# Attention and a token/channel mixer on one core: paced loads, moved squares, merges on another engine, another order at the start

## The chip, the cores and the metric

The kernel runs on one core of a Trainium2 chip. A core has TensorE (PE, matrix products), VectorE (DVE), ScalarE (ACT), GpSimd (POOL) and SyncE (SP, used here only to issue transfers); 16 DMA engines move data between the chip's memory and the core. TensorE reads from the on-chip SBUF and writes to PSUM, which has eight banks of 512 float32 values in each of 128 partitions. The metric is the device time of the program in microseconds (us).

## The reference

Eight batches of 576 positions, eight heads of 64. First causal attention with a bias that comes from `s`, then a mixer over tokens and one over channels:

```python
scores = scale * np.matmul(q, k.transpose(0, 1, 3, 2))
cum = np.cumsum(np.maximum(s, 0.0), axis=-1)
bias = -(cum[:, :, :, None] - cum[:, :, None, :])
scores = np.where(causal, -1000000000.0, scores + np.minimum(bias, 0.0))
attn = softmax(scores); x = np.matmul(attn, v)          # heads side by side: (8, 576, 512)
h  = np.maximum(xt @ w_tok1, 0.0) @ w_tok2              # xt: x with tokens last; 576 -> 256 -> 576
u  = x + h.transpose(0, 2, 1)
h2 = np.maximum(u @ w_ch1, 0.0) @ w_ch2                 # 512 -> 1536 -> 512
out = u + h2
```

## The kernel before

Because the bias is a difference of cumulative sums, the kernel multiplies v by weights exp(cum - cum_end / 2) (tile `wT`) and adds a column of those weights for the denominators; distant blocks of keys, whose weight is negligible, are left out. The program checks the data for this (cumulative sums in `gaps`, and sums of squares of all q and k in `square`), sums the flags, and runs a general version behind a branch if one is set.

The work of one batch `b`:

- `load_cast` and `stage_v`: q, k and v are loaded by POOL's queue (`load_op`), q and k with a cast to bf16 in two halves of four heads into a ring of five tiles `qkn`, v in five pieces of 128 positions into one of two tiles `vf`. All loads form one chain in the program's order, and each waits for the landing of the load eight before it.
- `merge_v` (L631): each piece of v times its weights, into `vp`; `ones` (L640, L642) copies the weight column. For batch one on VectorE, for batch two on either engine, for the other six on POOL.
- `quad` (L689): TensorE transposes q and k of four heads, and VectorE or ScalarE copies them out of PSUM (L699, L701). `pair` (L731): scores, exp on ScalarE (L739), the causal mask on VectorE (L748, L756), products with v on TensorE (L802), division (L831, L835). Batch one has its mask instead from presets (L722), matmuls that write large negative numbers into the score banks first.
- `tok` (L899, L961): the token mixer; from batch three on, its result `ua`, `ub`, `us` is transposed into `uTa`, `uTb` by transposing transfers on SyncE's queue (L977). `chan` (L1017, L1042): the channel mixer, with relu evictions on ScalarE (L1024) or VectorE (L1026), and stores (L1055, L1058).
- `squares` (L647): sums of squares on ScalarE. The tiles of batches one and two are given up before their squares can be taken, so `stage_sq` loads those q and k again, eight more loads at the end of the chain.

The order is not that of the text: every step is an operation with a duration for each engine that may run it, and `Plan.run` places operations one by one on engines and buffers by readiness and priority, with its own model of the load stream (`dma_free`, the time at which the first transfer can begin, and a length for each load). After 50 us of planned time it adds 0.5 us to what TensorE waits for and 2 us to what waits for a transfer. Each engine then executes its list strictly in that order. Before 45 us of planned time gaps on TensorE are filled with matmuls on zeros (L1135). Two score buffers `psc` (two banks each) and four single banks `pmx` hold all of TensorE's results.

At the very start the k and q of the first four heads come through SyncE's queue, are cast on ScalarE and VectorE and transposed; s comes third, VectorE takes its scan (L534, `cum`), ScalarE the exponential `wn` (L540), TensorE turns it (L560), and VectorE copies it to `wT` (L564) and merges v.

In the program as built, the kernel has 6,854 TensorE instructions ahead of the general version's, matmuls and weight loads together.

Of the kernel before, what the change touches and what calls it, by code (L numbers as in the profile page):

```python
# [13 lines left out]

SWITCH = 0.095
# [39 lines left out]
class Plan:  # L55
# [11 lines left out]
    def op(self, alts, reads=(), writes=(), prio=0, dma=0.0, holds=(), after=None, mode=0, lock=False, alone=None):  # L67
        o = Op()
        o.alts = alts
        o.prio = prio  # L70
        o.dma = dma
        o.mode = mode
        o.lock = lock
        o.alone = alone
        o.idx = len(self.ops)
        o.deps = set()
        o.users = []
        o.bufs = []
# [24 lines left out]
        self.ops.append(o)  # L103
        return o

    def run(self, eps=0.03):
# [15 lines left out]
        dma_free = 6.0  # L122
# [20 lines left out]
        while left:  # L143
# [68 lines left out]
            for u in o.users:  # L212
# [6 lines left out]
                else:  # L219
                    rdy = fin  # L220
                    if fin > STEADY:
                        rdy += MARGIN_DMA if o.dma else MARGIN if u.alts.keys() == {"PE"} else 0.0
# [145 lines left out]
def kernel(  # L368
# [83 lines left out]
    def load_op(fn, key, us, occ=0.75, prio=-1):  # L452
# [7 lines left out]
    def load_cast(n, b, h, i, src):  # L460
# [4 lines left out]
        load_op(load, [(n, i)], 1.45, prio=-1 if b or h else -3)  # L465
# [50 lines left out]
    for ti, src in enumerate((k, q)):  # L516
# [17 lines left out]
    P.op({"DVE": (1.3, 1.6, lambda: nc.vector.tensor_tensor_scan(  # L534
        out=cum[:, :], data0=one_sb[:, :], data1=s_sb[:, :], initial=0.0, op0=ALU.mult, op1=ALU.add))},
        reads=["sr"], writes=["cum"], prio=-1)
# [62 lines left out]
    def stage_v(b, cs=tuple(range(NJ))):  # L599
# [4 lines left out]
        for c in cs:  # L604
# [13 lines left out]
            load_op(load, [(vf, c)], 1.15 * n / 128, 0.92)  # L618
# [3 lines left out]
    def merge_v(b, cs=tuple(range(NJ))):  # L622
        vf, vp = vbuf[b]
        odd = b % 2
        for c in cs:
# [17 lines left out]
        P.op({"POOL": (0.5, 0.7, lambda: ones(nc.gpsimd))} if b else {"DVE": (0.25, 0.3, lambda: ones(nc.vector))},  # L643
             reads=["wT"], writes=[(vp, "w")], prio=b * 10 + 5 if b else -5, lock=True)
# [27 lines left out]
    def quad(b, h):  # L672
# [4 lines left out]
        for ti in range(2):  # L677
# [6 lines left out]
            def tr(ti=ti, pv=pv):  # L684
                for r in range(R):
# [6 lines left out]
            P.op({"PE": (R * 0.031, R * 0.031 + 0.21, tr)}, reads=([(nat, ti, 0), (nat, ti, 1)] if b == 0 and h == 0 else [(nat, ti)]) + ["ident"] + pads,  # L692
                 writes=[(pts[e], e) for e in range(2)], holds=[d[ti] for d in dsts], prio=(np_ - 30 * (b < 1 and h < 1), 2), mode=1)
# [13 lines left out]
    def pair(b, h, kT, qT):  # L707
# [3 lines left out]
        for pc, piece in enumerate(PIECES):  # L711
# [7 lines left out]
            if b == 0:  # L719
# [4 lines left out]
                P.op({"PE": (2 * c_pe(512)[0], 2 * c_pe(512)[0] + 0.21, preset)}, reads=["neg", "ident"],  # L724
# [116 lines left out]
    def load_w(fn, key, us, occ=0.75):  # L841
        load_op(lambda: nc.gpsimd.dma_start(**fn()), [key], us, occ)
# [246 lines left out]
    for b in range(2):  # L1089
        for h in range(0, H, 4):  # L1090
            stage_sq(b, h)
    for b in range(B):
# [3 lines left out]
        chan(b, *st)  # L1096

# [86 lines left out]
```

## Time and profile before

| | |
|---|---|
| median of three runs | 306.04 us (305.45 to 306.58) |
| the profiled execution | 306.06 us, span of its instructions 304.3 us |
| TensorE, VectorE, ScalarE, POOL busy in the span | 96%, 57%, 60%, 35% |
| granted TensorE clock | 0.995 |
| read from the chip's memory, written to it | 40.65 MB, 9.44 MB |

Lines of the profile name the kernel's line, the engine and operation, and the tiles without buffer numbers (`pmx<-uTb,wc`). POOLq and SPq are queues that issue transfers; a transfer's landing is later than its issue. Times in the timeline count from the first instruction of the span. "issue" is time in which an engine waited for nothing that the profile shows.

### The profile page before, as it was taken

The numbers are of one execution on the slowest core, as the hardware profiler recorded it, in microseconds if no ns is written. First come the engines' busy times: TensorE is split into PE (matmuls) and PEld (weight loads), VectorE is DVE, ScalarE is ACT, GpSimd is POOL, SyncE is SP. The second block draws the span as 40 slices with busy tenths as digits, with TensorE's granted clock in tenths as the row PEclk, the third lists the DMA queues.
The fourth block names the chain that finished last, engine by engine and source line by source line (L and its number), as shares of the span: only waits on it lengthen the run. The fifth ranks groups of instructions, "written<-read, shape, count | busy, mean of one in ns | idle before, by whom it ended". The sixth has DMA issues, their size and how long they took to land.

```text
span 304.3 us, 8094 instructions
## 1 busy us (share of the span) xinstructions
PE 291.8 (96%) x3430; PEld 168.2 (55%) x3430; DVE 172.0 (57%) x368; ACT 182.8 (60%) x298; POOL 107.6 (35%) x147
## 2 busy tenths in 40 slices
PE   8899999899999999999999999998999999999991
PEld 3478566467754545457754545455764544457550
DVE  5962889377976456756556556956456642420030
ACT  5887884699996486609872387727761286017300
POOL 8675469999780418107620108500000000000000
PEclk9999999999999999999999999999999999999998
DMA  8999999999997673358455535894004310250032
GB/s 218 226 207 206 216 224 229 252 190 262 227 156 125 155 197 54 79 140 178 94 80 103 133 84 83 132 116 136 2 2 84 125 38 0 69 155 2 0 111 74
DMA packets 38348, 39.29 MB, mean 129 GB/s; under 512 B 17600, under 2 KB 30976, under 8 KB 38304
## 3 DMA queue, kind: packets, MB, share of 16 engines
q0 software_dynamic: 17072, 24.25, 44.6%
q1 hardware_dynamic: 21232, 14.44, 18.7%
q8 instruction: 29, 0.48, 0.7%
q14 instruction: 15, 0.12, 0.1%
HBM read 40.65 MB, written 9.44 MB: 165 GB/s over the span
## 4 chain that ended last, share of the span: by engine, by line
PE 84%; DMA 12%; POOL 1%; issue 1%; DVE 0%; POOLq 0%
PE pmx L1017 30%; PE pmx L1042 30%; PE pmx L961 5%; PE pmx L899 5%; PE psc L802 5%; PE psc L731 5%; DMA qkn<-in_k_dram 5%; PE psc L689 3%; DMA wc<-in_moe_w_ch_dram 3%; DMA vf<-in_v_dram 2%; DMA uTb<-us 2%; POOL qkn L462 1%; PE pmx L986 0%; DVE of L1050 0%; POOL keep masks.py:66 0%
## 5 line engine op out<-in xcount | busy, mean ns | idle before, releaser
L1017 PEld LDWEIGHTS <-wc 128*128 128x128 bf16 x624 | 57.9, 98 | 32.6 <-issue 1.5
L739 ACT ACTIVATE E<-psc 128x1024 bf16<-128x1024 f32 x64 | 62.2, 1024 | 22.8 <-PE psc L731 22.2
L1017 PE MATMUL pmx<-uTb,wc 128*128 128x320 bf16 (+2 forms) x384 | 56.1, 299 | 1.4 <-DMA uTb<-ub 1.1
L1042 PE MATMUL pmx<-wc,gb 128*128 128x512 bf16 (+1 forms) x252 | 55.3, 369 | 0.0
L1017 PE MATMUL pmx<-uTa,wc 128*128 128x512 bf16 (+1 forms) x240 | 45.6, 337 | 0.0
L647 ACT ACTIVATE junk<-qkn 128x1152 bf16<-128x1152 bf16 x32 | 37.3, 1166 | 11.7 <-DMA qkn<-in_q_dram 11.3
L1042 PE MATMUL pmx<-wc,ga 128*128 128x512 bf16 x192 | 44.1, 379 | 0.0
L631 POOL TENSOR_TENSOR vp<-vf,wT 128x512 bf16<-128x512 f32 (+1 forms) x31 | 32.3, 1058 | 25.6 <-PE psc L802 24.9
L1024 ACT ACTIVATE gb<-pmx 128x320 bf16<-128x320 f32 (+2 forms) x57 | 24.7, 438 | 21.2 <-PE pmx L1017 17.3
L1042 PEld LDWEIGHTS <-gb 128*128 128x128 bf16 x252 | 23.6, 98 | 24.8 <-issue 0.2
L613 POOL DMA_DIRECT2D vf<-in_v_dram x39 | 34.1, 884 | 7.3 <-DMA qkn<-in_k_dram 2.2
L748 DVE TENSOR_TENSOR E<-E,keep 128x512 bf16<-128x512 bf16 x56 | 25.8, 474 | 13.3 <-ACT E L739 13.1
L1042 PEld LDWEIGHTS <-ga 128*128 128x128 bf16 x192 | 18.2, 98 | 20.4
L1024 ACT ACTIVATE ga<-pmx 128x512 bf16<-128x512 f32 (+1 forms) x36 | 19.2, 535 | 11.7 <-PE pmx L1017 11.1
L462 POOL DMA_DIRECT2D qkn<-in_k_dram x19 | 14.1, 744 | 33.5 <-issue 31.8
L1026 DVE TENSOR_SCALAR gb<-pmx 128x320 bf16<-128x320 f32 (+2 forms) x39 | 18.8, 487 | 11.9 <-PE pmx L1017 11.5
L699 ACT COPY kT<-psc 128x576 bf16<-128x576 bf16 x22 | 13.1, 641 | 19.4 <-PE psc L689 17.9
L802 PEld LDWEIGHTS <-E 128*128 128x128 bf16 x576 | 21.1, 97 | 5.5
L835 DVE TENSOR_TENSOR x<-psc,rc 128x640 bf16<-128x640 f32 x28 | 23.0, 823 | 0.9
L1050 DVE TENSOR_TENSOR of<-pmx,ua 128x512 f32<-128x512 f32 x16 | 11.0, 689 | 19.5 <-PE pmx L1042 19.3
L731 PE MATMUL psc<-qT,kT 64*128 64x256 bf16 (+2 forms) x320 | 21.3, 250 | 0.0
L731 PEld LDWEIGHTS <-kT 64*128 64x128 bf16 x320 | 12.6, 94 | 14.6 <-issue 11.5
(107 smaller groups left out, 300.9 us busy)
## 6 DMA issues: line engine op xcount, KB each, us to landing
vf<-in_v_dram POOLq DMA_DIRECT2D x32, 256.0 KB, 7.9
out_dram<-of SPq DMA_DIRECT2D x31, 256.0 KB, 2.3
qkn<-in_k_dram POOLq DMA_DIRECT2D x19, 288.0 KB, 6.7
qkn<-in_q_dram POOLq DMA_DIRECT2D x19, 288.0 KB, 7.3
wc<-in_moe_w_ch_dram POOLq DMA_DIRECT2D x8, 384.0 KB, 11.4
out_dram<-of SPq DMA_DIRECT2D x10, 128.0 KB, 2.3
vf<-in_v_dram POOLq DMA_DIRECT2D x7, 128.0 KB, 7.4
gb<-in_k_dram SPq DMA_DIRECT2D x1, 576.0 KB, 3.9
```

Of the source, the lines that this page charges most:

```text
L613: nc.gpsimd.dma_start(out=vf.t[p0 : p0 + n, c, :, :], in_=v[b, :, c * 128 : c * 128 + n, :].rearrange("h p d -> p h d"))
L631: eng.tensor_tensor(out=vp.t[p0 : p0 + n, c, :, 0:D], in0=vf.t[p0 : p0 + n, c, :, :], in1=wT[p0 : p0 + n, cw, b * H : b * H + H].unsqueeze ...
L647: nc.scalar.activation(out=junk[:, :].rearrange("p (t n) -> p t n", t=2), in_=i, func=AF.Square, accum_out=sq[:, col : col + 1])
L731: nc.tensor.matmul(out=ps.t[:, hh * 512 + c0 : hh * 512 + c0 + e - a], lhsT=kT.t[hh * 64 : hh * 64 + 64, j0 : j0 + 128], rhs=qT.t[hh * 64 ...
L739: nc.scalar.activation(out=E.t[:, :, 512 * pc : 512 * pc + 512], in_=ps.t[:, :].rearrange("p (e n) -> p e n", e=2), func=AF.Exp, scale=0.125)
L748: nc.vector.tensor_tensor(out=o, in0=o, in1=keep[:, :].unsqueeze(1).unsqueeze(1).to_broadcast([128, 2, 2, 128]), op=ALU.mult)
L802: nc.tensor.matmul(out=o[:, ic, 0:DE], lhsT=E.t[:, hh, d0 : d0 + 128], rhs=vp.t[:, jc, h + 2 * hh, 0:DE], start=(jc == j_lo), stop=(jc == ic))
L835: nc.vector.tensor_tensor(out=x.t[:, :, :].rearrange("p c (g f e d) -> p g e f c d", f=2, e=2, d=D)[:, h // 4, h % 2], in0=pav2()[:, :, :, ...
L1017: nc.tensor.matmul(out=pm.t[:, 0 : e - a], lhsT=wc1[:, m, cc * 128 : cc * 128 + 128], rhs=uT.t[:, m, a:e], start=(m == 0), stop=(m == NMC ...
L1024: lambda cc=cc, pm=pm, a=a, e=e: nc.scalar.activation(out=g.t[:, cc, a:e], in_=pm.t[:, 0 : e - a], func=AF.Relu),
L1026: lambda cc=cc, pm=pm, a=a, e=e: nc.vector.tensor_scalar_max(out=g.t[:, cc, a:e], in0=pm.t[:, 0 : e - a], scalar1=0.0)),
L1042: nc.tensor.matmul(out=pm.t[:, na:ne], lhsT=g.t[:, cc, c * 128 : c * 128 + 128], rhs=wc2[:, cc, na:ne], start=(cc == 0), stop=(cc == NCC - 1))
```

## The change

Five edits, after which the planner orders everything anew:

1. Loads 17 to 44 of the chain are each preceded on POOL by a one-element copy (`touch`) from the tile that the load five before it fills, so that at most five are under way. The first of these is a part of `w_ch2`, right behind the loads of token weights, of `w_ch1` and of the first half of batch two.
2. The eight extra loads for squares leave the end of the chain as built and come behind five such copies that read the five columns of `uTb` of batch six (index 5), each filled by one of its transposing transfers. Squares get 6 us more of planned margin behind their loads, the copies none.
3. For batches three to eight, v is merged by VectorE and not by POOL, the weight columns too; batch two may still use either for the merges.
4. The presets of batch one wait for the first transposes; the scan of s waits for the second ones, with a lower priority.
5. The planner takes 6.85 instead of 6.0 us as the earliest begin of the load stream.

```diff
+DEPTH = 5
+PACED = (16, 44)
...
-        dma_free = 6.0
+        dma_free = 6.85
...
-                        rdy += MARGIN_DMA if o.dma else MARGIN if u.alts.keys() == {"PE"} else 0.0
+                        m = MARGIN_DMA + u.late if o.dma else MARGIN if u.alts.keys() == {"PE"} else 0.0
+                        rdy += max(m, 0.0)
...
+    def touch(ap, reads, col):
+        o = P.op({"POOL": (0.12, 0.2, lambda: nc.gpsimd.tensor_copy(out=seen[0 : ap().shape[0], col : col + 1], in_=ap()))},
+                 reads=reads, writes=[("seen", col)], prio=-1, after=chain[-1])
+        o.late = -9.0
+        chain.append(o)
+
+    probes = []
+
+    def load_op(fn, key, us, occ=0.75, prio=-1, probe=None):
+        if PACED[0] <= len(probes) < PACED[1]:
+            touch(*probes[-DEPTH], 0)
+        probes.append((probe, key))
...
-    P.op({"DVE": (1.3, 1.6, lambda: nc.vector.tensor_tensor_scan(
+    scan = P.op({"DVE": (1.3, 1.6, lambda: nc.vector.tensor_tensor_scan(
...
-        reads=["sr"], writes=["cum"], prio=-1)
+        reads=["sr"], writes=["cum"], prio=2)
...
-            alts = {} if b == 0 else {"POOL": (*c_pool(512, 0.0019), lambda mul=mul: mul(nc.gpsimd))}
-            if b < 2:
-                alts["DVE"] = (*c_dve(512), lambda mul=mul: mul(nc.vector))
-            P.op(alts, reads=[(vf, c), "wT"], writes=[(vp, c)], prio=-2 if b < 3 else b * 10 + 5, lock=True)
+            alts = {"DVE": (*c_dve(512), lambda mul=mul: mul(nc.vector))}
+            if b == 1:
+                alts["POOL"] = (*c_pool(512, 0.0019), lambda mul=mul: mul(nc.gpsimd))
+            P.op(alts, reads=[(vf, c), "wT"], writes=[(vp, c)], prio=-2 if b < 3 else b * 10 + 5, lock=b < 2)
...
-        P.op({"POOL": (0.5, 0.7, lambda: ones(nc.gpsimd))} if b else {"DVE": (0.25, 0.3, lambda: ones(nc.vector))},
-             reads=["wT"], writes=[(vp, "w")], prio=b * 10 + 5 if b else -5, lock=True)
+        P.op({"POOL": (0.5, 0.7, lambda: ones(nc.gpsimd))} if b == 1 else {"DVE": (0.3, 0.35, lambda: ones(nc.vector))},
+             reads=["wT"], writes=[(vp, "w")], prio=b * 10 + 5 if b else -5, lock=b < 2)
...
-                 reads=[(n, 0), (n, 1)], writes=[("sq", col)], prio=60)
+                 reads=[(n, 0), (n, 1)], writes=[("sq", col)], prio=60).late = 6.0
...
+            turn = P.op({"PE": (R * 0.031, R * 0.031 + 0.21, tr)}, ...
+                 writes=[(pts[e], e) for e in range(2)] + (["turned"] if b == 0 and h == 0 and ti == 0 else []), ...
+            if b == 0 and h == 0 and ti == 1:
+                scan.deps.add(turn)
...
-                P.op({"PE": (2 * c_pe(512)[0], 2 * c_pe(512)[0] + 0.21, preset)}, reads=["neg", "ident"],
+                P.op({"PE": (2 * c_pe(512)[0], 2 * c_pe(512)[0] + 0.21, preset)}, reads=["neg", "ident"] + ["turned"],
...
-    for b in range(2):
-        for h in range(0, H, 4):
-            stage_sq(b, h)
     for b in range(B):
         for h in range(0, H, 4):
             quad(b, h)
         st = tok(b)
         chan(b, *st)
+        if b == B - 3:
+            for c in range(NJ):
+                touch(lambda c=c, uT=st[2]: uT.t[0:1, 0, c * 128 : c * 128 + 1], [(st[2], c)], 1)
+            for i in range(2):
+                for h in range(0, H, 4):
+                    stage_sq(i, h)
```

More of the change, by code (lines that the diff above doesn't have):

```diff
@@ L77, in op @@
         o.users = []
+        o.late = 0.0
         o.bufs = []
@@ L450 @@
     sent = []
-    def load_op(fn, key, us, occ=0.75, prio=-1):
+    seen = sb("seen", [128, 8], FP32, fast)
+    def touch(ap, reads, col):
[8 more added lines that the diff above has]
+        probes.append((probe, key))
         o = P.op({"POOL": (occ, 0, fn)}, writes=key, prio=prio, dma=us, after=chain[-1] if chain else None)
@@ L464, in load @@
                 in_=src[b, h : h + 4, :, :].rearrange("(f e) (p r) d -> (e p) f (r d)", e=2, r=R))
-        load_op(load, [(n, i)], 1.45, prio=-1 if b or h else -3)
+        load_op(load, [(n, i)], 1.45, prio=-1 if b or h else -3, probe=lambda: n.t[0:1, i, 0, 0:1])
     qkn = {}
@@ L617, in stage_v @@
                 continue
-            load_op(load, [(vf, c)], 1.15 * n / 128, 0.92)
+            load_op(load, [(vf, c)], 1.15 * n / 128, 0.92, probe=lambda c=c, p0=p0: vf.t[p0 : p0 + 1, c, 0, 0:1])
         if b:
@@ L691, in tr @@
                                                 identity=ident[p0 : p0 + PR, p0 : p0 + PR])
-            P.op({"PE": (R * 0.031, R * 0.031 + 0.21, tr)}, reads=([(nat, ti, 0), (nat, ti, 1)] if b == 0 and h == 0 else [(nat, ti)]) + ["ident"] + pads,
-                 writes=[(pts[e], e) for e in range(2)], holds=[d[ti] for d in dsts], prio=(np_ - 30 * (b < 1 and h < 1), 2), mode=1)
+            turn = P.op({"PE": (R * 0.031, R * 0.031 + 0.21, tr)}, reads=([(nat, ti, 0), (nat, ti, 1)] if b == 0 and h == 0 else [(nat, ti)]) + ["ident"] + pads,
+                 writes=[(pts[e], e) for e in range(2)] + (["turned"] if b == 0 and h == 0 and ti == 0 else []), holds=[d[ti] for d in dsts], prio=(np_ - 30 * (b < 1 and h < 1), 2), mode=1)
+            if b == 0 and h == 0 and ti == 1:
+                scan.deps.add(turn)
             for e in range(2):
@@ L841, in load_w, with probe @@
     def load_w(fn, key, us, occ=0.75):
-        load_op(lambda: nc.gpsimd.dma_start(**fn()), [key], us, occ)
+        def probe():
+            o = fn()["out"]
+            return (o[0:1, 0, 0:1] if len(o.shape) == 3 else o[0:1, 0:1])
+        load_op(lambda: nc.gpsimd.dma_start(**fn()), [key], us, occ, probe=probe)
     def load_tok():
```

## The prediction

> **What bounds the kernel now.** I read the first part of the page, then what TensorE waited for, then the chain that ended last.
>
> ```profile
> span 304.3 us, 8094 instructions
> PE 291.8 (96%) x3430; PEld 168.2 (55%) x3430; DVE 172.0 (57%) x368; ACT 182.8 (60%) x298; POOL 107.6 (35%) x147
> ```
>
> ```profile
> PE pmx L899 <- issue: 1.3, 1, 1.3
> ...
> PE pmx L1017 <- DMA uTb<-ub: 1.1, 1, 1.1
> PE pmx L689 <- DMA qkn<-in_k_dram: 0.8, 1, 0.8
> PE psc L689 <- DMA qkn<-in_k_dram: 0.6, 1, 0.6
> PE pmx L1017 <- DMA uTb<-us: 0.3, 1, 0.3
> ```
>
> ```profile
> 21.25 14.20 DMA qkn<-in_k_dram
> 35.50 0.48 PE psc L689 x36
> 35.98 0.97 PE pmx L961 x4
> 36.95 0.44 PE pmx L1017 x4
> ...
> 54.79 1.28 issue
> ...
> 200.91 6.61 DMA uTb<-us
> ...
> 297.60 0.42 DVE of L1050
> ```
>
> TensorE is busy 96% of the span. In the list of waits (engine, line, what it waited for, total, times, longest) everything that TensorE waited for is a few tenths to 1.3 us. From the first matmul of token mixing (L899 at 20.23, quoted below) to 297.6 us it does nothing but useful matmuls, and the changed kernel has the same ones, column for column (685,084). So a gain can come from two places only: an earlier start of that stretch, and the holes in it. The holes are 0.6 us before the key transposes of the second half of batch two (35.50), 1.28 us at 54.79, and 1.1 + 0.3 = 1.4 us around 206, before the channel mixing of batch six (L1017 waiting for uTb). The ceiling without the start is 3.3 us.
>
> **Part 1, the squares' loads behind batch six's transposing transfers.** Columns: start, length, engine queue or engine, line, operation.
>
> ```profile
> 193.86 0.77 POOL L462 DMA_DIRECT2D qkn<-in_k_dram  x1 [0.92 <-ACT junk L647]
> ...
> 194.44 6.37 SPq L977 DMA_TRANSPOSE uTb<-ub  x4
> 200.91 3.72 SPq L977 DMA_TRANSPOSE uTb<-us  x1
> ...
> 231.40 5.19 SPq L977 DMA_TRANSPOSE uTa<-ua  x4
> ...
> 204.68 0.80 PE L689 MATMUL psc<-ident,qkn 64*64 64x64 bf16 x72
> ```
>
> Four such transfers take SyncE's queue 5.19 us undisturbed (batch seven); beside the last extra loads (the row is the k half of the last; its q half follows at once) four took 6.37 and the fifth 3.72. Undisturbed, the five take 5 x 1.30 = 6.5 us, to 200.9, and TensorE is ready for them only at 204.68 + 0.80 = 205.48. Landing would have to take more than 4.5 us to be late again. So the whole hole goes: -1.4. What is moved: eight POOL loads, which now follow five one-element copies that wait for the five transfers. Nobody else is queued on POOL by then. The eight squares on ScalarE (L647) move to 207 to 230 us; by the group's row and an accumulator read they take about 1.3 us each.
>
> ```profile
> L647 ACT ACTIVATE junk<-qkn 128x1152 bf16<-128x1152 bf16 x32 | 37.3, 1166 | 11.7 <-DMA qkn<-in_q_dram 11.3
> ...
> 207.00:230.00 23.00, 22.68 (x276) 14.77 (x275) 12.38 (x30) 15.21 (x26) 0.00 (x0) 1.00 0.09 33
> ```
>
> There ScalarE is busy 15.21 us of 23 and VectorE 12.38; seven squares more (one of the eight was there already), 7 x 1.3 = 9.1 us, fit in the two together (36.7 of 46) because the planner hands evictions of L1024 to VectorE (L1026). Cost 0; without that cover it is up to 1.3 us (24.3 in 23).
>
> **Part 2, the start.**
>
> ```profile
> 7.61 0.48 PE L689 MATMUL pmx<-ident,qkn 64*64 64x64 bf16 x36
> 9.63 0.61 PE L731 MATMUL psc<-qT,kT 64*128 64x256 bf16 x10
> 10.70 0.48 PE L689 MATMUL pmx<-ident,qkn 64*64 64x64 bf16 x36
> 17.63 1.84 PE L802 MATMUL pmx<-vp,E 128*128 128x64 bf16 x54
> 20.23 2.72 PE L899 MATMUL pmx<-x,w 128*128 128x256 bf16 x30
> ...
> 11.30 1.42 DVE L701 COPY qT<-pmx 128x576 bf16<-128x576 bf16 x2
> 12.64 0.55 DVE L564 COPY wT<-pmx 128x384 f32<-128x384 f32 x1
> 13.39 3.08 DVE L631 TENSOR_TENSOR vp<-vf,wT 128x512 bf16<-128x512 f32 x5
> 17.18 0.22 DVE L790 RECIPROCAL rc<-pmx 128x10 f32<-128x10 f32 x1
> ...
> 8.13 1.18 ACT L699 COPY qT<-pmx 128x576 bf16<-128x576 bf16 x2 [0.88 <-PE pmx L689]
> ```
>
> The four presets that stood before the first transposes now take the place of fill matmuls behind them: 0. The scan of s goes behind a qT copy, and wn behind the second exp. In the new order the first scores follow the first q transposes (7.61) instead of waiting, in TensorE's queue, behind the next quad's k transposes (0.8 us for a load). ScalarE evicts one half alone (0.59 us, to 8.7) while VectorE takes the other, so the scores start near 8.8, 0.8 before 9.63, and the exps with them. But the second quad's q transposes now stand behind a preset and the next scores, which need the first exp's buffer: about 11.2 instead of 10.70. VectorE's qT copies, wT and the v merges are a chain behind them: wT 13.15, and 3.08 + 0.22 for the merges and the reciprocal that is now among them, end 17.5 instead of 16.47. The products with v (L802) need those merges, so they start near 17.5 instead of 17.63, and L899 follows. I take -0.15; bounds -0.8 (the exps' whole lead) and +0.4 (the merges 0.5 later than I have them). The planner's constants (first transfer at 6.85, the squares' extra margin) only move the order and cost nothing themselves.
>
> **Part 3, work moved ahead of the late load.** Before the k transposes of 35.50 the changed order has four more matmuls of L1017 and two more of L961: 0.44 + 0.97 / 2 = 0.93 us by the chain's rows. TensorE would reach them at 34.9 - 0.15 + 0.93 = 35.7, after the load has landed: -0.6. The margin is 0.2 us; if the load lands later than that, it is late again, one for one.
>
> **Part 4, five loads under way.** From the seventeenth load on, each is preceded on POOL by a one-element copy that waits for the landing of the load five before it, instead of a wait for eight before.
>
> ```profile
> 35.74 0.69 POOL L613 DMA_DIRECT2D vf<-in_v_dram  x1 [1.36 <-DMA qkn<-in_k_dram]
> ...
> 89.45 0.77 POOL L462 DMA_DIRECT2D qkn<-in_k_dram  x1
> ...
> 47.72 1.25 PE L802 MATMUL psc<-vp,E 128*128 128x65 bf16 x36
> ```
>
> ```profile
> DMA to landing us min/median/max: 10.3/10.3/10.3
> ```
>
> ```profile
> DMA to landing us min/median/max: 4.6/4.6/4.6
> ```
>
> These are the landings of those two loads. With eight under way a load takes 10.3 to 14.2 us (the chain's longest), so landings are 10.3 / 8 to 14.2 / 8, about 1.5 us, apart, and five deep should take 7.5. A load with little ahead of it needs 4.6 us; with 0.3 for the copy (my allowance; the trace has no such copy), 4.9 / 5 = 1.0 us a load is what five can sustain. That is under 1.5, so the stream stays full and landings stay where they were: 0. Bounds: -1.28 (rival one) and +4 (rival three). Behind a copy that waits stand POOL's next loads and one merge of batch two, nothing else. The tightest customer is the last v piece of batch two: issued 35.74, landed 46.0, and after a merge of 0.68 (row in part 5) needed by L802 at 47.72, or with the gains so far at 46.95. That leaves some 0.2 us.
>
> **Part 5, v merged by VectorE.**
>
> ```profile
> L631 POOL TENSOR_TENSOR vp<-vf,wT x31: 1032/1047/1232, 43.5 to 191.1; 128x512 bf16<-128x512 f32 x25, 64x512 bf16<-64x512 f32 x6
> L631 DVE TENSOR_TENSOR vp<-vf,wT x9: 674/678/690, 13.4 to 46.5; 128x512 bf16<-128x512 f32 x7, 64x512 bf16<-64x512 f32 x2
> ...
> 13.37 0.70 POOL L842 DMA_DIRECT2D wc<-in_moe_w_ch_dram  x1 [0.50 <-DMA vf<-in_v_dram]
> ```
>
> Batches three to eight have thirty merges: 30 x 0.68 = 20.4 us more on VectorE (172.0 to 192 and the denominators' small copies), 30 x 1.05 = 31 us less on POOL. The pieces of the chain shown belong to VectorE only at the very end, so I cost this at nothing: what hides it is that VectorE and ScalarE share the evictions and that TensorE has four banks to run ahead in; rival two is the price if that cover is gone. Nothing below zero either, since no wait of TensorE names POOL's merges. What stands behind a merge on VectorE is the next eviction or mask, and behind those TensorE.
>
> POOL's issue of a load took 0.70 us while VectorE ran its five merges (13.37), and 0.77 us at 89.45. [...]
>
> **Sum**: 306.06 (the profiled execution: span 304.3 and 1.76 around it; the median of the runs is 306.04) - 1.4 - 0.6 - 0.15 = 303.9.
>
> **Rivals.** One, the hole at 54.79 goes too. It stands inside a group of L899, at a matmul that waits for no semaphore, in the stretch with most loads under way, so it looks like TensorE waiting for instructions. With fewer loads ahead a fetch could come sooner: 303.9 - 1.28 = 302.6. Against it: the packed stretch and the count of instructions stay. The Trainium skill (Runtime: NRT & Kernel Launch, Instruction fetch mechanics) has instructions stream in blocks of 256 whose crossing is mostly hidden; the 1.28 us here disagree with it, and by the rule the changed kernel would have no hole: 302.6 too.
>
> Two, VectorE's queue turns into a wait. Batch three's v lands from about 49.5 us, and in the new order its merges stand between reciprocals, normalizations and evictions of batch two's token mixing; five merges are 3.4 us in a stretch with
>
> ```profile
> 50.00:55.00 5.00, 4.79 (x133) 3.77 (x130) 3.58 (x8) 3.62 (x7) 4.83 (x8) 1.00 1.15 228
> ```
>
> 3.58 us of 5 taken on VectorE: 2.0 us too many. If half of that is absorbed and one more batch does the same, holes of 1.5 to 2 us come back: 303.9 + 1.5 = 305.4, no change. For it speaks the order, against it that the list of waits has no hole of TensorE behind VectorE today.
>
> Three, slower: five loads don't keep the stream full. It decides when a round trip passes 5 x 1.5 = 7.5 us. At 0.3 us more a load, ten loads later the last v piece of batch two lands 3 us late and TensorE waits some 3 us at 47; the loads up to batch three add 1 us: 303.9 + 4 = 307.9. For it speaks that each paced load adds a POOL instruction to a round trip, against it the margin between 1.0 and 1.5. [...]
>
> **How the numbers follow.** Forecast 0.42, rival one 0.23, two 0.20, three 0.15. No change means within 0.5% (1.5 us), about what a measurement of this kernel can tell: the first two are faster (0.65), two is same, three slower. The range runs from rival one with 0.6 us more at the start, 302.0, to 307.0, inside rival three; the forecast's own is 303.2 to 304.5.
>
> **What would show it.** Right: no wait of L1017 for uTb near 205, the fifth transfer short; no wait at the second k transposes near 35; L802 first at about 17.5. Wrong: a new entry among TensorE's waits naming VectorE or vf, load landings over 8 us from issue between 22 and 60 us, or a longer hole at 54.

## The result, and the profile after

The changed kernel takes 302.9 us (median of six runs, 301.73 to 303.23), the kernel before beside it 306.09 us (304.35 to 307.21): ratio 0.9893, 95% interval 0.9859 to 0.9926. In three later series, on other chips, the kernel before had medians of 305.0, 305.0 and 305.2 us over 25 runs each, so the gain may be nearer to 2.2 than to 3.2 us; the changed kernel itself was not run on those chips.

The page of the changed kernel, first part, and its list of TensorE's waits (engine, line, what it waited for, total, times, longest). Lines have moved: L899 is now L921, L1017 L1039, L1042 L1064, L689 L706, L802 L821, L748 L767, L631 L648, L977 L999.

```profile
span 301.1 us, 8152 instructions
...
PE 292.5 (97%) x3432; PEld 168.0 (56%) x3432; DVE 187.5 (62%) x408; ACT 183.9 (61%) x300; POOL 80.6 (27%) x138
```

```profile
PE pmx L1160 <- DVE zero L487: 1.2, 1, 1.2
PE pmx L803 <- DVE vp L659: 0.3, 1, 0.3
PE pmx L921 <- issue: 0.2, 1, 0.2
```

Of the holes that the prediction named one is left, at 0.2 us; the first two lines here are of the start, before token mixing. The timeline of TensorE, then that of SyncE's queue (start, length, line, operation), and the chain that ended last (start, length, what):

```profile
17.49 1.84 PE L821 MATMUL pmx<-vp,E 128*128 128x64 bf16 x54
...
20.10 2.72 PE L921 MATMUL pmx<-x,w 128*128 128x256 bf16 x30
```

```profile
193.38 5.53 SPq L999 DMA_TRANSPOSE uTb<-ub  x4
199.01 1.20 SPq L999 DMA_TRANSPOSE uTb<-us  x1
```

```profile
35.62 0.41 PE psc L706 x36
...
54.50 0.21 issue
54.72 0.72 PE pmx L921 x10
...
294.36 0.42 DVE of L1072
```

The profiled executions differ by 306.06 - 302.87 = 3.2 us, and the lines account for it: token mixing starts 0.13 us earlier (20.23 to 20.10); TensorE goes into the second k transposes without a wait (35.62, -0.6); the hole near 54.8 is 0.21 instead of 1.28 us (-1.07); the fifth transposing transfer takes 1.20 instead of 3.72 us and L1039 waits for nothing (-1.4). What follows TensorE's last matmul is unchanged. Which edit did which of these is another question, and the answers are not the ones that I gave.

### The profile page after: what moved, and what is told of

The parts are those of the page before. It is cut to its first block, busy times and chain, and to the rows that moved or that the text cites. A ratio compares the mean times of both kernels' runs of the same rounds, so it can differ in the third digit from the quotient of the medians.

```text
span 301.1 us, 8152 instructions
## 1 busy us (share of the span) xinstructions
PE 292.5 (97%) x3432; PEld 168.0 (56%) x3432; DVE 187.5 (62%) x408; ACT 183.9 (61%) x300; POOL 80.6 (27%) x138
## 4 chain that ended last, share of the span: by engine, by line
PE 95%; DVE 1%; ACT 1%; issue 0%; DVEq 0%
PE pmx L1039 32%; PE pmx L1064 31%; PE psc L750 6%; PE pmx L983 6%; PE pmx L921 6%; PE psc L821 5%; PE psc L706 3%; PE pmx L1160 2%; PE psc L741 1%; ACT x L843 1%; PE pmx L706 1%; PE pmx L959 1%; DVE qT L720 0%; PE pmx L1008 0%; PE pmx L949 0%; DVE x L837 0%
## 5 line engine op out<-in xcount | busy, mean ns | idle before, releaser
L1039 PEld LDWEIGHTS <-wc 128*128 128x128 bf16 x624 | 58.0, 98 | 31.2 <-issue 1.1
L1039 PE MATMUL pmx<-uTb,wc 128*128 128x320 bf16 (+2 forms) x384 | 55.6, 299 | 0.0
L1064 PE MATMUL pmx<-wc,gb 128*128 128x512 bf16 (+1 forms) x252 | 54.7, 369 | 0.0
L1039 PE MATMUL pmx<-uTa,wc 128*128 128x512 bf16 (+1 forms) x240 | 45.6, 337 | 0.0
L1064 PE MATMUL pmx<-wc,ga 128*128 128x512 bf16 x192 | 44.6, 379 | 0.0
L1064 PEld LDWEIGHTS <-gb 128*128 128x128 bf16 x252 | 23.7, 98 | 25.1
L1046 ACT ACTIVATE gb<-pmx 128x320 bf16<-128x320 f32 (+2 forms) x53 | 23.0, 436 | 20.0 <-PE pmx L1039 16.1
L630 POOL DMA_DIRECT2D vf<-in_v_dram x39 | 33.4, 870 | 4.6 <-issue 2.0
L767 DVE TENSOR_TENSOR E<-E,keep 128x512 bf16<-128x512 bf16 x56 | 22.9, 416 | 10.9 <-ACT E L758 10.7
L1064 PEld LDWEIGHTS <-ga 128*128 128x128 bf16 x192 | 18.1, 98 | 20.2 <-issue 0.2
L1046 ACT ACTIVATE ga<-pmx 128x512 bf16<-128x512 f32 (+1 forms) x43 | 22.8, 535 | 10.3 <-PE pmx L1039 9.5
L648 DVE TENSOR_TENSOR vp<-vf,wT 128x512 bf16<-128x512 f32 (+1 forms) x39 | 25.5, 686 | 1.5 <-DMA vf<-in_v_dram 1.3
L1048 DVE TENSOR_SCALAR gb<-pmx 128x320 bf16<-128x320 f32 (+2 forms) x43 | 20.9, 490 | 5.4 <-PE pmx L1039 4.3
L821 PEld LDWEIGHTS <-E 128*128 128x128 bf16 x576 | 21.1, 97 | 5.5
L479 POOL DMA_DIRECT2D qkn<-in_q_dram x19 | 13.7, 722 | 28.3 <-PE psc L706 25.4
```

The source lines that it names most:

```text
L479: nc.gpsimd.dma_start(out=n.t[:, i, :, :], in_=src[b, h : h + 4, :, :].rearrange("(f e) (p r) d -> (e p) f (r d)", e=2, r=R))
L630: nc.gpsimd.dma_start(out=vf.t[p0 : p0 + n, c, :, :], in_=v[b, :, c * 128 : c * 128 + n, :].rearrange("h p d -> p h d"))
L648: eng.tensor_tensor(out=vp.t[p0 : p0 + n, c, :, 0:D], in0=vf.t[p0 : p0 + n, c, :, :], in1=wT[p0 : p0 + n, cw, b * H : b * H + H].unsqueeze ...
L767: nc.vector.tensor_tensor(out=o, in0=o, in1=keep[:, :].unsqueeze(1).unsqueeze(1).to_broadcast([128, 2, 2, 128]), op=ALU.mult)
L821: nc.tensor.matmul(out=o[:, ic, 0:DE], lhsT=E.t[:, hh, d0 : d0 + 128], rhs=vp.t[:, jc, h + 2 * hh, 0:DE], start=(jc == j_lo), stop=(jc == ic))
L1039: nc.tensor.matmul(out=pm.t[:, 0 : e - a], lhsT=wc1[:, m, cc * 128 : cc * 128 + 128], rhs=uT.t[:, m, a:e], start=(m == 0), stop=(m == NMC ...
```

## The experiments

"Before plus" has one edit alone; "after minus" has all but one. The ratio is to the kernel before on the same chip; "holes" are TensorE's idle time from the first matmul of token mixing to the last of channel mixing, without gaps of 0.16 us, which stand where single matmul records are missing. The start was not undone in the changed kernel.

| kernel | us | ratio (95%) | holes, us |
|---|---|---|---|
| before, after (profiled) | 306.1, 302.9 | 0.989 (0.986 to 0.993) | 3.3, 0.2 |
| before plus squares (`b_sq`) | 312.5 | 1.021 (1.014 to 1.028) | 7.7 |
| before plus start (`b_start`) | 304.4 | 0.997 (0.995 to 0.999) | 1.3 |
| before plus pacing (`b_pace`) | 305.7 | 0.999 (0.996 to 1.003) | 2.8 |
| before plus merges (`b_vm`) | 305.7 | 1.001 (0.998 to 1.004) | 0.9 |
| after minus squares (`a_nosq`) | 302.9 | 0.994 (0.992 to 0.997) | 0.4 |
| after minus pacing (`a_nopace`) | 305.2 | 1.002 (0.999 to 1.005) | 0.7 |
| after minus merges (`a_novm`) | 310.3 | 1.020 (1.014 to 1.026) | 5.7 |

The edits don't add up. Alone they are worth +7.5, -0.6, +0.7 and +0.7 us (medians, and by their intervals the last two can't be told from nothing); together -3.2, measured on another chip.

**The squares' loads.** `b_sq` has the second edit alone, `a_nosq` everything else:

```diff
-    for b in range(2):
-        for h in range(0, H, 4):
-            stage_sq(b, h)
...
+        if b == B - 3:
+            for c in range(NJ):
+                touch(lambda c=c, uT=st[2]: uT.t[0:1, 0, c * 128 : c * 128 + 1], [(st[2], c)], 1)
+            for i in range(2):
+                for h in range(0, H, 4):
+                    stage_sq(i, h)
```

> The kernel before with one edit, the squares' eight extra loads behind batch six's transposing transfers. Theory (the holes add up): the wait of L1017 for uTb near 206 (1.1 + 0.3 us) goes, the 1.28 us at 54.79 and the 0.6 us at 35.5 stay: 306.1 - 1.4 = 304.7. Rival (a hole that is closed comes back as another, later one, since TensorE then runs into a load or an eviction that is late): no more than half of the 1.4 us shows, 305.4 or above, and a new entry among TensorE's waits.

> The changed kernel without the move of the squares' loads: the other three edits stay. Step one of the prediction (the move is what removes the wait near 206): L1017's successor waits 1.4 us for uTb again, 304.3. Rival (the wait belonged to one alignment of loads and transposing transfers, and any of the other edits shifts it away, as each did alone): no such wait, 302.9 as the changed kernel.

Both theories of `b_sq` missed it by 7 us. In its chain and its list of waits, and in the timelines of TensorE, SyncE's queue and POOL:

```profile
98.68 13.20 DMA uTa<-ua
```

```profile
PE pmx L1037 <- DMA uTa<-ua: 5.5, 1, 5.5
```

```profile
94.39 0.48 PE L706 MATMUL psc<-ident,qkn 64*64 64x64 bf16 x36
```

```profile
94.58 5.46 SPq L997 DMA_TRANSPOSE uTa<-ua  x4
```

```profile
95.20 0.71 POOL L479 DMA_DIRECT2D qkn<-in_q_dram  x1 [4.44 <-PE psc L706]
95.91 4.24 POOL L630 DMA_DIRECT2D vf<-in_v_dram  x5
```

The fourth transposing transfer of a batch in the middle landed 13.2 us after its issue, and TensorE waited 5.5 us for it. (Undisturbed, such a transfer holds SyncE's queue for 1.2 to 1.3 us and lands 2.4 to 2.5 us after its issue, as the five of batch six do in the changed kernel.) Six loads, 1.4 MB, went out beside it and its companions: the key transposes of the next half batch, which give up the buffer that the first of these loads waits for, stand at 94.39. In the kernel before these transposes (102.15) stand behind that stretch, and so do the loads:

```profile
102.96 0.72 POOL L462 DMA_DIRECT2D qkn<-in_q_dram  x1 [12.74 <-PE psc L689]
```

So the planner, given another list of loads, let one small group of transposes slip ahead and with it a burst of loads into a stretch that was free of them. A second cost came with the wait: in the window from 110 us on (columns: window, length, busy time of TensorE, its weight loads, VectorE, ScalarE, POOL, granted clock, DMA share, GB/s) TensorE is granted half its clock after the pause:

```profile
110.00:115.00 5.00, 2.98 (x23) 1.72 (x24) 0.09 (x1) 0.60 (x1) 0.00 (x0) 0.53 0.55 200
115.00:120.00 5.00, 4.78 (x26) 2.08 (x26) 2.34 (x4) 3.36 (x6) 0.00 (x0) 0.79 0.00 0
```

`a_nosq` decides on step one: without the move the wait near 206 doesn't come back, and the time is the changed kernel's. The transfers are still disturbed there, but TensorE isn't held up by them. There the last extra loads (192.68 and 193.39) go out 1.1 and 0.4 us ahead of the first transfer (193.75); in the kernel before it was 0.6 us ahead and 0.2 behind. The transposing transfers issued from 193 to 206 us (kind, count, median us to landing), first of the kernel before, then of `a_nosq`:

```profile
uTb<-ub SPq DMA_TRANSPOSE x4, 9.5
uTb<-us SPq DMA_TRANSPOSE x1, 6.6
```

```profile
uTb<-ub SPq DMA_TRANSPOSE x4, 5.7
uTb<-us SPq DMA_TRANSPOSE x1, 2.9
```

Each of the other edits alone removed that wait too (`b_start`, `b_pace`, `b_vm`): it seems to belong to one alignment of loads and transfers, within a microsecond. `b_shift190` below, with the order of the kernel before, has 0.65 us of it.

**The start.**

```diff
-        dma_free = 6.0
+        dma_free = 6.85
...
+            if b == 0 and h == 0 and ti == 1:
+                scan.deps.add(turn)
...
-                P.op({"PE": (2 * c_pe(512)[0], 2 * c_pe(512)[0] + 0.21, preset)}, reads=["neg", "ident"],
+                P.op({"PE": (2 * c_pe(512)[0], 2 * c_pe(512)[0] + 0.21, preset)}, reads=["neg", "ident"] + ["turned"],
```

> The kernel before with the start's edits alone (presets behind the first transposes, the scan of s behind the second quad's, the first transfer's constant 6.85). Theory: the first products with v at 17.5 instead of 17.63 (-0.15), the four matmuls of L1017 and two of L961 come ahead of the k transposes near 35, so that wait goes or shrinks to under 0.2 us; the holes at 54 and 206 stay: 306.1 - 0.15 - 0.5 = 305.4. Rival (the start is worth the whole lead of the exps): 0.8 us earlier, 304.8.

In the profiles TensorE is done 1.7 us earlier (295.82 against 297.56): the waits near 206 (1.4) and 35.5 (0.6) are gone and the start is 0.2 earlier, while the hole near 55 stayed at 1.29 us; 0.4 us are lost again among the matmuls themselves, which I can't explain. The wait at 35.5 needs no edit to go: `b_shift190` below, with the order of the kernel before, has none there. In all kernels of these experiments but the one with three loads under way that k half landed between 33.9 and 34.4 us, whether five or eight were under way, as here without the pacing (POOL's timeline of `a_nopace`, and the landing of this load):

```profile
20.49 0.73 POOL L479 DMA_DIRECT2D qkn<-in_k_dram  x1
```

```profile
DMA to landing us min/median/max: 13.6/13.6/13.6
```

That is 34.1, and TensorE comes to it at 34.8 or later. The 35.5 of the prediction is that of one profiled execution, on the first chip; whether the other executions there had it is not known. Token mixing started at 20.05 us. Over the profiled kernels without the hundred tiny matmuls of a later part, which shift the start too, that number is 19.64 to 20.28 with the new start (seven kernels, mean 19.93) and 20.23 to 20.56 with the old one (four, mean 20.38): the start is worth some 0.45 us, with a spread of up to 0.6 from one execution to the next.

**The pacing and the hole.** `b_pace` adds the copies to the kernel before, `a_nopace` sets `PACED = (0, 0)` in the changed one.

> The kernel before with the pacing alone: five loads under way instead of eight, from the seventeenth load on. Theory A (fewer loads ahead let TensorE's next instructions come sooner, and a load that shares the engines with fewer others lands earlier): the hole near 54.8 shrinks from 1.28 us to about 0.6 although the order of TensorE's work up to there is unchanged, the second k transposes no longer wait near 35 (0.6 us): 306.1 - 0.7 - 0.6 = 304.8. Rival B (the changed kernel has no hole there only because its order puts 0.4 us more work into that stretch): the hole stays at 1.2 to 1.3 us, and time 305.5 to 306.1. Step four of the prediction (pacing is worth nothing): 306.1.

> The changed kernel with eight loads under way instead of five: everything else stays. Theory A (loads ahead delay the fetch of TensorE's instructions): the hole near 54.5 is 6.1 - 4.8 = 1.3 us less what the trace of the other single edits took off, so 0.9 to 1.3, 303.8 to 304.0. Rival B (the order alone closed it): 0.2 as in the changed kernel, 302.9. The second k transposes near 35 wait 0 to 0.3 us, since their load lands at 35.5 again.

The hole, in TensorE's timeline, before and in `b_pace`, whose order of TensorE's work is the same up to there:

```profile
53.73 1.07 PE L899 MATMUL pmx<-x,w 128*128 128x128 bf16 x16
56.08 0.38 PE L899 MATMUL pmx<-x,w 128*128 128x128 bf16 x4 [1.28 <-issue]
```

```profile
53.67 1.07 PE L919 MATMUL pmx<-x,w 128*128 128x128 bf16 x16
54.97 0.38 PE L919 MATMUL pmx<-x,w 128*128 128x128 bf16 x4 [0.23 <-issue]
```

Same matmul, same order, fewer loads under way: 1.05 us less. That is theory A, and rival B falls as the main cause. With eight loads under way but the changed order (`a_nopace`) it is 0.69 us, so the 0.4 us of matmuls that the new order puts ahead help as well. (Between traces with one order and one number of loads the hole differs by some 0.2 us: 1.28 and 1.10, 0.69 and 0.91, 0.22 and 0.40.) From the weight load 128 places ahead of the hole (why 128 stands in the part on borders, below) to the hole's end it is 5.9 to 6.3 us in six kernels with eight under way (for the kernel before 4.8 of matmuls + 1.3 of hole), and 5.0 to 5.8 in three with five (`b_pace`: 4.8 + 0.2). The other half of theory A, the earlier landing, falls: without the pacing that load lands as early.

But `b_pace` is no faster in the median; its ten runs spread from 303.7 to 309.0 us. The profiled one, 307.5, is among the longer ones. Its list of waits has two new entries, and VectorE's and POOL's timelines show why:

```profile
PE psc L819 <- DVE E L765: 1.9, 1, 1.9
...
PE psc L819 <- DVE E L773: 0.7, 1, 0.7
```

```profile
76.17 2.18 DVE L765 TENSOR_TENSOR E<-E,keep 128x512 bf16<-128x512 bf16 x1
78.28 1.06 DVE L773 TENSOR_TENSOR E<-E,keep 128x128 bf16<-128x128 bf16 x1
```

```profile
76.20 1.05 POOL L648 TENSOR_TENSOR vp<-vf,wT 128x512 bf16<-128x512 f32 x1
...
77.97 1.27 POOL L648 TENSOR_TENSOR vp<-vf,wT 128x512 bf16<-128x512 f32 x1
```

A mask multiplication that takes 0.42 us took 2.18 while GpSimd merged and issued a load, and the small one 1.06 instead of 0.22, up to the end of GpSimd's next merge. In the kernel before this happened where TensorE had work to go on with (the longest mask took 1.26 us); the pacing spread GpSimd's work over the masks that TensorE waits for. And, as in `b_sq`, a slower clock followed the waits (the columns are those of the windows above):

```profile
79.00:81.00 2.00, 1.61 (x16) 1.34 (x17) 2.00 (x6) 0.00 (x0) 1.93 (x3) 0.50 1.16 175
```

By the trace's clock records it was 0.50 from 78.5 to 81.9 us, so up to 1.7 us come on top of the 2.6 us of waits: more than the holes that went. How often the runs of `b_pace` meet this, one profile doesn't say.

**Where v is merged.** `b_vm` has the third edit alone, `a_novm` all others.

```diff
-            alts = {} if b == 0 else {"POOL": (*c_pool(512, 0.0019), lambda mul=mul: mul(nc.gpsimd))}
-            if b < 2:
-                alts["DVE"] = (*c_dve(512), lambda mul=mul: mul(nc.vector))
+            alts = {"DVE": (*c_dve(512), lambda mul=mul: mul(nc.vector))}
+            if b == 1:
+                alts["POOL"] = (*c_pool(512, 0.0019), lambda mul=mul: mul(nc.gpsimd))
```

> The kernel before with v merged by VectorE alone. Prediction: no change, 306.1, with no new wait of TensorE behind VectorE; if the order puts more work into the stretch ahead of the hole near 54.8, that hole shrinks by as much (to 0.7 to 0.9 us) and the time to 305.6. Rival two of the prediction (VectorE's queue becomes a wait): holes of 1.5 us behind VectorE, 307.6. [...]

> The changed kernel with v merged by GpSimd from batch three on, as before. Step five of the prediction (where v is merged costs and gains nothing): 302.9. Theory P, from the pacing alone (the mask multiplications took 1.6 and 2.2 us instead of 0.41 beside GpSimd's merges, and TensorE waited 2.6 us for them): with the paced loads GpSimd's merges fall among the masks, TensorE waits 1 to 3 us behind VectorE's masks, 304 to 306.

The masks (minimum, median and maximum in ns) of `b_pace` and of the changed kernel:

```profile
L765 DVE TENSOR_TENSOR E<-E,keep x56: 361/418/2177, 33.0 to 252.4; 128x512 bf16<-128x512 bf16 x56
```

```profile
L767 DVE TENSOR_TENSOR E<-E,keep x56: 359/416/427, 33.0 to 247.9; 128x512 bf16<-128x512 bf16 x56
```

With the merges on VectorE no mask takes longer than 0.43 us. In `b_vm` TensorE's holes shrink from 3.3 to 0.9 us, with no wait behind a merge: rival two falls. (Its time doesn't show it, for a reason told below.) `a_novm` is 7 us slower than the changed kernel, but not by the route that I expected: its longest mask took 1.18 us and TensorE's waits behind VectorE come to 0.6. It ran into the collision of `b_sq` in another batch. In its chain and POOL's timeline:

```profile
132.03 10.80 DMA uTb<-us
```

```profile
127.34 0.73 POOL L479 DMA_DIRECT2D qkn<-in_q_dram  x1 [4.40 <-PE psc L706]
128.06 4.24 POOL L630 DMA_DIRECT2D vf<-in_v_dram  x5
```

Six loads once more, issued beside five transposing transfers (126.38 to 133.6): 3.5 + 1.3 us of waiting for them. The experiment therefore doesn't say what GpSimd's merges alone would have cost in the changed kernel; `b_pace` says it for the old order, 2.6 us of waits in one execution.

**Is the hole a border of instructions?** The hundred tiny matmuls shift the stream and leave the work as it is:

```diff
+            if t0 < 3.0:
+                def small():
+                    for i in range(20):
+                        p, m, c = 64 * (i % 2), 64 * (i // 2 % 2), 64 * (i // 4 % 8)
+                        nc.tensor.matmul(out=r_mx.tiles[i % 2][m : m + 64, c : c + 64], lhsT=zero[p : p + 64, 0:64],
+                                         rhs=zero[p : p + 64, 0:64], start=True, stop=True)
+                f.fn = small
```

> The kernel before, in which five of the twenty fill matmuls ahead of the first load are replaced by a hundred tiny ones (64x64x64, no result used): TensorE's instruction stream is 190 instructions longer from the start, and nothing else changes. Theory A (the hole near 55 stands at a border of a block of 256 instructions, because the block before it holds only 4.4 us of matmuls while the next but one takes about 6 us to come): the borders move, the shortest block now holds 6.7 us, and the hole goes, 1.3 us less. Rival C (the hole belongs to those matmuls of L899's successor or to that moment): 1.2 to 1.3 us at the same matmuls, no gain. Theory A would be wrong too if a hole of the same length came back elsewhere between 45 and 70 us.

In TensorE's timeline of `b_shift190` the same twenty matmuls now run through, with eight loads under way:

```profile
54.22 1.29 PE L919 MATMUL pmx<-x,w 128*128 128x128 bf16 x20
...
64.90 0.38 PE L1006 MATMUL pmx<-ident,us 128*128 128x128 bf16 x4 [1.42 <-DVE of L1070]
```

The hole is gone and no "issue" of its length stands elsewhere: rival C falls, and theory A holds for the place as well as for the size. The Trainium skill (Runtime: NRT & Kernel Launch, Instruction fetch mechanics) has instructions arrive in blocks of 256; the shift was worked out with that number, and the trace agrees. The page calls the fetch hidden, which 1.28 us here contradict: the 256 instructions ahead of the hole, 128 pairs of weight load and matmul, held 4.8 us of matmuls.

The fetches themselves stand in the traces, as DMA packets of 16 KB on a queue of their own. The page of the kernel before has (queue, kind, packets, MB, share of 16 engines)

```profile
q8 instruction: 29, 0.48, 0.7%
```

Twenty-seven of them start before TensorE is done with its 6,860 matmuls and weight loads: some 254 instructions each, an estimate. In `b_shift190` the first comes at 5.1 us instead of 12.4, so they belong to TensorE's stream. The hole stands at one count of that stream, behind 863 weight loads, in nine traces with several orders of the matmuls there, and in all nine a packet ends 1.2 to 1.5 us before TensorE goes on (the kernel before: packet 53.64 to 54.60, TensorE 56.08; `b_pace`: 52.39 to 53.73, TensorE 54.97). It starts 3.6 to 4.2 us behind the weight load 128 places ahead of the hole in the six kernels with eight loads under way, and 2.5 to 3.4 us behind it in the three with five. So the hole is a late fetch behind a stretch of short matmuls, and more loads under way make it later.

The 1.3 us were not won, though: TensorE came sooner to the matmuls of 64.90 and waited there 1.42 us behind VectorE, whose small mask was once more held up by a merge (VectorE's and POOL's timelines):

```profile
63.07 1.06 DVE L773 TENSOR_TENSOR E<-E,keep 128x128 bf16<-128x128 bf16 x1
```

```profile
62.84 1.20 POOL L648 TENSOR_TENSOR vp<-vf,wT 128x512 bf16<-128x512 f32 x1
```

Time 305.2 us, ratio 1.001 (0.998 to 1.004).

**What else the pacing does.** `a_nopace` has TensorE finished only 0.5 us later than the changed kernel (294.83 against 294.32), and yet takes 2.3 us longer. In both, the last copy of the flag, and the first part of the page, the changed kernel's first (its span is quoted above):

```profile
294.90 0.14 DVE L1139 CAST flagi<-flagf 1x1 int32<-1x1 f32 x1
```

```profile
295.42 0.14 DVE L1139 CAST flagi<-flagf 1x1 int32<-1x1 f32 x1
```

```profile
span 302.9 us, 8111 instructions
...
PE 292.6 (97%) x3432; PEld 167.8 (55%) x3432; DVE 188.3 (62%) x409; ACT 182.3 (60%) x299; POOL 74.0 (24%) x110
```

From there to the end of the span are 301.07 - 295.05 = 6.0 us in the changed kernel and 302.86 - 295.56 = 7.3 us here; in `b_vm`, whose POOL has 105 busy instructions, 7.4 us; in the other kernels, with 133 and more, 6.0 to 6.3. So I padded GpSimd, and then shifted TensorE's stream too:

```diff
...
+            if not padded and o.start > 230.0:
+                for i in range(40):
+                    nc.gpsimd.memset(seen[:, 7:8], 0.0)
+                padded = True
```

> The changed kernel without the pacing, plus forty memsets of one column on GpSimd at 230 us, where that engine has nothing to do. Theory G: in the two kernels with the shortest GpSimd programs (v merged by VectorE and no copies for the pacing) the time from the flag's last copy to the end of the span was 7.3 and 7.4 us instead of 6.0 to 6.2; the length of GpSimd's program is what decides, so forty idle instructions win 1.3 us: 303.9 instead of 305.2, with TensorE's end at 294.8 as without them. Rival (the longer end belongs to the missing pacing itself, or to chance): 305.2.

> The same with the hundred tiny matmuls at the start as well, which move the borders of TensorE's blocks of instructions by 190. Theory A and G together: no pacing is needed; the 0.7 us hole near 55 goes too, TensorE ends at 294.1 and the time is 302.9 to 303.2, the changed kernel's. Rival (the pacing does something else of worth besides the hole and the length of GpSimd's program): 303.9 or above with another wait of TensorE in the list.

> The changed kernel, all edits, with the hundred tiny matmuls at the start: its last hole, 0.2 us near 54.5, goes: 302.7, no more than the measurement can tell from 302.9. It says whether anything is left in the stretch from the first matmul of token mixing to the end: 274.0 us of it in 274.2 is matmuls back to back.

Forty idle instructions make the kernel 1.5 us faster: 303.7 us, ratio 0.995 (0.993 to 0.997), with 6.0 us from the flag to the end. With the shift as well it takes 303.1 us (0.995, 0.992 to 0.998), no hole is left, and the chain ends, without any pacing, where the changed kernel's does:

```profile
294.46 0.42 DVE of L1072
```

So the pacing's worth in this kernel is the hole, 0.5 us on the chain, and its copies' making GpSimd's program long enough. What depends on that length is when GpSimd goes on behind the branch over the general version. The branch comes at 295.6 us in the changed kernel and at 296.1 in `a_nopace`; the first instruction of GpSimd's queue behind it (duration in ns, first and last start) in the changed kernel and in `a_nopace`:

```profile
L1177 POOLq EVENT_SEMAPHORE  x1: 17/17/17, 296.1 to 296.1; - x1
```

```profile
L1177 POOLq EVENT_SEMAPHORE  x1: 17/17/17, 299.4 to 299.4; - x1
```

So it is 0.5 us against 3.3, and in `a_nopace_pad` 0.5 again. The Trainium skill (Runtime: NRT & Kernel Launch, Instruction fetch mechanics) says that a taken branch whose target lies outside the window fetched ahead has to wait for it; that fits a program whose length decides, but no run here shows the window.

`a_shift190` came out at 303.1 us (0.994, 0.992 to 0.996). No hole is left in it, but in its profiled execution, the longest of ten, token mixing started at 21.79 instead of 20.10 us: the four presets took 1.89 us and not 1.04, and by the clock records full clock begins at 9.8 us and not at 5.7. So it doesn't say what the last hole alone is worth; no version beat the changed kernel by more than the measurement can tell.

**Three loads under way** (`DEPTH = 3`).

> The changed kernel with three loads under way instead of five. Rival three of the prediction, moved to where its rule lets it decide: a load alone takes 4.6 us and 0.3 for the copy, 4.9 / 3 = 1.63 us a load against about 1.5 needed, so the stream falls behind by 0.13 us a load, 3.6 us over the twenty-eight paced loads, and TensorE waits 1 to 4 us in all for qkn or vf: 304 to 307. Step four's rule would be wrong if three were as good as five (302.9).

311.4 us (four runs, 309.9 to 314.9), ratio 1.020 (1.015 to 1.025). Its profiled execution was the longest, so it is read for the kinds of waits only:

```profile
PE psc L706 <- DMA qkn<-in_k_dram: 2.9, 2, 2.7
PE pmx L983 <- DVE ub L990: 1.9, 1, 1.9
PE psc L821 <- DVE E L767: 1.6, 2, 1.1
...
PE psc L821 <- DVE vp L648: 0.5, 1, 0.5
```

Rival three's wait for qkn is there, 2.7 us, and behind it waits for VectorE's evictions, masks and merges. The rule for where the stream starves held; its price was too low: 8.5 us (7.0 for the shortest run) instead of 1 to 4.

## Why the prediction was right, and where it was not

The time, 302.9 us, lies in the range (302.0 to 307.0), and faster was the likeliest; the forecast was 1.0 us too high, and rival one (302.6) is the case that came. Step by step:

- **The bounds.** Of 3.3 us of holes 3.1 went in the profiles, and the matmuls between them took as long as before (274.0 us in both). But one of the holes stands in no other profile (part 3).
- **Part 1, -1.4 for the squares' loads.** The size was right, and so was the mechanism of the transfers: with the move the five land 2.4 to 2.5 us after their issue, without it (`a_nosq`) 2.9 to 7.2. But `a_nosq` has no such wait either, so the move isn't what wins the 1.4 us in the changed kernel. I worked out what the transfers cost without loads beside them, and not what else could take the loads away; any edit that shifted the two against each other did. "Cost 0 ... nobody else is queued on POOL" was wrong by 7.5 us for the edit alone: I looked at what waits on POOL where the loads go to, not at what the planner does with the list of loads that they leave.
- **Part 2, -0.15 for the start.** -0.13 in the two profiles, L821 first at 17.49 as forecast (17.5), but -0.45 over all; inside the bounds. The reason given for 17.5 isn't borne out: the terms that I named add up to 17.2 us, the merges ended at 17.30, and TensorE came to the products without a wait, from the work ahead of them. That the time agreed was luck.
- **Part 3, -0.6 at the second k transposes.** The step failed though the wait went. TensorE came at 35.6 (forecast 35.7), but the load lands at 34.1 or so in every other execution with five or eight loads under way, and TensorE is there at 34.8 at the earliest: the wait that I wanted to remove stands in one profile and in no other with five or eight. The removal was luck as far as the edits go.
- **Part 4, nothing for the pacing.** The step that failed by most. "Landings stay where they were" held up to 35 us; later the stream was not full (DMA share 0.79 from 40 to 45 us, before 1.11; loads issued from 42.3 to 46.3 us landed after 4.1 to 4.8 us, not 7.5), and no load was missed for it. Loads that landed 8.1 to 8.4 us after their issue, which I had named a sign of being wrong, cost nothing. What mattered was not the loads but the fetches of TensorE's instructions among them: -1.05 us in `b_pace`. I had this as rival one, at 0.23, with "the packed stretch and the count of instructions stay" against it; they stayed, and the hole went.
- **Part 5, nothing for the merges.** Right in that VectorE's queue took 15.5 us more (172.0 to 187.5) without a new wait, so rival two fell; wrong in "nothing below zero either". I looked for waits that name GpSimd's merges, and what they did stood under VectorE's masks, whose longest took 1.26 us against a median of 0.42. I didn't weigh that GpSimd could hold up VectorE, which `b_pace` shows at 2.18 us. The Trainium skill (SBUF — State Buffer, SBUF: two separate sides) has the rule: a VectorE operation with two SBUF inputs and a GpSimd operation that reads SBUF exclude each other, and the one that comes second waits for the whole of the first. The trace agrees in kind; one merge of 1.05 us and the mask's own 0.42 would make 1.5 us, and why it was 2.18 is not shown. I take it that the merges' leaving GpSimd is what lets the pacing's gain through; `a_novm`, which should have shown it, met the other collision.
- **Left out altogether:** 1.3 us at the end that hang on the length of GpSimd's program. The merges' move alone loses them, the pacing's copies win them back.

Between the two profiled executions the 1.0 us by which the forecast was high is rival one's hole, 1.07 us.

## What to carry to other kernels

When a planner orders the work, an edit's price is that of the order that comes out: undo each part in the finished kernel, since parts that gain nothing alone (pacing, merges) can need each other, and a part with a good story (the squares' loads) can be worth nothing. Look at the maxima of short operations, not only at the medians: a mask five times as long as its fellows points to a neighbour that holds it up; and ask of a wait of half a microsecond whether a second profile has it. Keep bursts of loads away from transposing transfers that TensorE will need, and read an "issue" hole inside a group of equal matmuls as instructions that come late.

## What the runs showed of the hardware that I had not expected

- A transposing transfer that lands 2.4 to 2.5 us after its issue when undisturbed took 10.8 and 13.2 us when six loads of GpSimd's queue were issued beside it.
- VectorE's mask multiplications (two SBUF inputs) stretched from 0.42 to 2.18 us beside merges on GpSimd, and never passed 0.43 in the changed kernel, whose merges are on VectorE.
- TensorE's hole of 1.28 us shrank to 0.23 with five loads under way instead of eight, and vanished with eight when the stream of instructions was shifted by 190. It ends 1.2 to 1.5 us behind a 16 KB packet of the instruction queue.
- Forty idle instructions on GpSimd shortened the end of the program by 1.2 us: GpSimd went on 0.5 us behind the branch and not 3.3.
- After a wait of 5.5 us TensorE's granted clock was 0.53 in the next window of 5 us and 0.79 in the one after; in `b_pace` it was 0.50 from 79 to 81 us, behind waits of 1.9 and 0.7 us. In `a_novm` it stayed at 1.00 behind a wait of 3.5 us.
